# Loading the first key tile over ScalarE's queue, twelve products of ones on TensorE, and the first values ahead of the second pair

## The chip, the cores and the metric

The kernel runs on one core of one Trainium2 chip. The metric is the device time of one execution in microseconds (us). A core has engines that run side by side, each through its own list of instructions in order: TensorE (PE in the profile, its weight loads PEld), VectorE (DVE), ScalarE (ACT), GpSimd (POOL) and SyncE (SP). SyncE issues nearly all DMAs of this kernel; what it issues is carried out by 16 DMA engines. An engine waits for another one, or for a DMA, on a semaphore.

## The reference

```python
scores = np.matmul(q, k.transpose(0, 1, 3, 2)) / 8
scores = cap * np.tanh(scores / cap)
scores = scores - np.max(scores, axis=-1, keepdims=True)
attn = np.exp(scores)
attn = attn / (np.sum(attn, axis=-1, keepdims=True) + 1e-09)
x = np.matmul(attn, v)                  # (8, 12, 448, 64), then heads side by side: (8, 448, 768)
gate_pre[:, s] = sum over i of conv_w[i] * xp[:, s + i]      # xp is x with 4 zero rows ahead of it
out = (sigmoid(gate_pre) * (x @ w_val)) @ w_out
```

q, k and v are (8, 12, 448, 64) in float32; w_val and w_out (768 x 768) and conv_w (5 x 768) come as float64 and are taken apart into two float32 parts on the chip. cap is one number.

## The kernel before

Two heads make a pair p; there are 48 pairs, 6 in each of the 8 batches. For each pair, `load_blocks` (L165) brings q and k in four DMAs each, 32 rows of 14 blocks of 32 numbers a DMA, and `turn` (L289, its transposition L291) transposes them on VectorE, so that the 64 numbers of each of the two heads lie on partitions (`qt`, `kt`). The keys are cut into four tiles of 112. `scores` (L312) makes the scores of one key tile for both heads (`pss`, 112 x 896) with two matmuls side by side, each of which TensorE runs in two passes; `tanh` (L320) and `exp` (L324) are one ScalarE instruction each over such a tile; `attnv` (L349) multiplies by the values `vn`, which `load_v` (L184) brings in two DMAs, and `sums` (L361) by `ones`, which gives the sums of the softmax. Then VectorE turns the sums (`zt`, L369), inverts them and multiplies (`u`, L390), ScalarE copies the result (`xh`, L395), and the convolution (`gate`), the sigmoid and the two large products (`val`, `out_part`) follow.

Two score tiles fit into PSUM at a time (`ps_s` has two buffers). The work of all pairs is written in one order, sorted by due times: a table gives each step of pair p the time p + x, and the sorted list is what each engine executes, in order. The tables of the first six pairs (`EARLY`) put `scores` of pair p ahead of the end of pair p - 1. Into the same order come the weights: step n loads a piece of w_val or w_out (`weight_load`, `late_load`: `w_raw` and `w_late`), and takes it apart with two instructions on ScalarE (`weight_first`, L126 and L127) and several on VectorE (L130, L131, L134 to L136). The first of these steps is due at 0.70, and so stands on ScalarE behind the four `exp` of pair 0 and ahead of the `tanh` of pair 1. The small weights conv_w (`cw_raw`, five DMAs) stand just ahead of it.

The start is apart from this order. Ahead of it the kernel loads cap (`capt`) and the q and k of pair 0 (into `u2`, two buffers that are free until pair 0 is done: u0 for q and u1 for k), computes a flag from cap (`mag`, `small`), and every engine reads the flag (`TENSOR_LOAD`) and branches to `fast_path`. All other DMAs are issued behind the branch. A DMA reports on one of eight semaphores (DMAHW0 to DMAHW7), which are handed out in turn; an issue waits until the earlier DMA on its semaphore has landed.

Of the kernel before, what the change touches and what calls it, by code (L numbers as in the profile page):

```python
# [7 lines left out]
F32 = mybir.dt.float32  # L8
# [13 lines left out]
P = 128  # L22
ENG = mybir.EngineType

CH = 112
# [73 lines left out]
W_SECOND, W_THIRD, W_THIRD_EARLY = 0.02, 0.05, 0.71  # L99
W_FREE = 11.3  # L100
CW_LOAD, CW_AT = -0.55, 0.6
EPS = 1e-9


# [57 lines left out]
    return make  # L162


def load_blocks(nc, t, src, p):  # L165


    _, H, S, D = src.shape
    b, hp = divmod(p, H // 2)
    for g in range(P // BLK):  # L170
        j, d = divmod(g * BLK, D)
        nc.sync.dma_start(
            t[g * BLK:(g + 1) * BLK].rearrange("p (c e) -> p c e", e=BLK),
            src[b, 2 * hp + j, :, d:d + BLK].rearrange("(c r) e -> r c e", r=BLK),
        )


# [7 lines left out]
    return vn  # L185


def fast_path(tc, io, u2, q, k, v, w_val, conv_w, w_out, out, capt):

# [19 lines left out]
    with ExitStack() as ctx:  # L211
# [21 lines left out]
        nc.vector.scalar_tensor_tensor(guard, capt, -1.0, capt, ALU.mult, ALU.min)  # L233
        nc.scalar.activation(guard, guard, AF.Exp)
        nc.vector.tensor_scalar_mul(guard, guard, EPS)  # L235
        ones = cpool.tile([P, D], F32, name="ones")
        nc.gpsimd.memset(ones, 1.0)
        cw = cpool.tile([P, NCC, KW], F32, name="cw")

        for t in u2:  # L240
# [43 lines left out]
        def load(name, src, p):  # L284
            if p:
                loads[name, p] = io.tile([P, S], F32, name=name + "n")
                load_blocks(nc, loads[name, p], src, p)

        def turn(name, p):  # L289
            t = wk.tile([P, S], F32, name=name + "t")  # L290
            nc.vector.transpose(t, loads.pop((name, p)))  # L291
            state.setdefault(p, {})[name] = t

        def half_hi(name, p):
# [58 lines left out]
        def sums(p, i):  # L353

            st = state[p]
            n = len(tables[p]["sums"])
            if i == 0:
                st["z"] = bank(p, "psz")
            t = st["p" if n == NKT else "a", i]
            for j, r in enumerate(ROWS):  # L360
                nc.tensor.matmul(st["z"][r, :S], ones[:CH], t[:, j], start=(i == 0), stop=(i == n - 1))  # L361
            if i == n - 1:
                vloads.pop(p)

# [131 lines left out]
        for p, table in enumerate(tables):  # L496
            for name, f in steps.items():
                x = table.get(name, ())
                if isinstance(x, tuple):
                    for i, y in enumerate(x):  # L500
                        at(p + y, f, p, i)
                else:
                    at(p + x, f, p)
        for b in range(B):
            t0 = NPAIR * b
            for d in range(NCC):
# [157 lines left out]
def kernel(tc, q, k, v, cap, w_val, conv_w, w_out, out):  # L664
    nc = tc.nc
    with tc.tile_pool(name="cap_pool", bufs=1) as pool, tc.tile_pool(name="io", bufs=2) as io:
        capt = pool.tile([P, 1], F32, name="capt")
        nc.sync.dma_start(capt, cap.rearrange("(o c) -> o c", o=1).partition_broadcast(P))

        pad = conv_w.shape[0] - 1  # L670
        u2 = [pool.tile([P, pad + q.shape[2]], F32, name=f"u{i}") for i in range(2)]
        for t, src in zip(u2, (q, k)):
            load_blocks(nc, t[:, pad:], src, 0)
        mag = pool.tile([1, 1], F32, name="mag")
        nc.vector.scalar_tensor_tensor(mag, capt[0:1], -1.0, capt[0:1], ALU.mult, ALU.max)
        small = pool.tile([1, 1], I32, name="small")
        nc.vector.tensor_scalar(small, mag, CAP_FAST, None, ALU.is_le)
        flag = nc.values_load(small, min_val=0, max_val=1)
        with tc.If(flag != 0) as cmp:
            fast_path(tc, io, u2, q, k, v, w_val, conv_w, w_out, out, capt)  # L680
        with cmp.Else():
            general_path(tc, q, k, v, w_val, conv_w, w_out, out, capt)

# [29 lines left out]
```

## Time and profile before

| | |
|---|---|
| median of 3 runs | 750.18 us (749.81, 750.18, 752.12) |
| the profiled execution | 749.64 us |
| its span in the profile, from the first to the last instruction | 747.9 us |
| TensorE matmuls | busy 724.3 us, 97% of the span |
| VectorE | 593.0 us, 79% |
| ScalarE | 537.7 us, 72% |
| DMA, mean over the span | 85 GB/s; 241820 packets, 228448 of them under 512 B |

The profile is of one execution. Busy shares are averages over the whole span; the change touches the first 15 us, in which the engines stand in other proportions. All times that follow are counted from the start of the span. In rows of the timeline a bracket at the end gives how long the engine was idle ahead of the instruction and what released it by the profile's reading.

### The profile page before, as it was taken

The page shows a single profiled execution, that of the slowest core. Times are in us where ns is not written, and L with a number is a line of the kernel's source. Part 1 is how long each engine was busy: PE and PEld are TensorE (multiplying, and loading weights), DVE is VectorE, ACT ScalarE, POOL GpSimd, SP SyncE. Part 2 cuts the span into 40 slices and gives each one's busy share as a digit, 9 for nine tenths or more (in the row PEclk, how much of TensorE's full clock was granted, in tenths as well). Part 3 has the DMA queues.
Part 4 walks back from the last instruction along what each step waited for, and adds up shares of the span by engine and source line. Part 5 has one row for each costly group of instructions (what it writes and reads, how often), then busy time and mean ns, then how long its engine had stood idle before and what let it go on. Part 6 is the DMA issues. An engine that isn't in the chain of part 4 may idle for free.

```text
span 747.9 us, 10860 instructions
## 1 busy us (share of the span) xinstructions
PE 724.3 (97%) x3972; PEld 488.3 (65%) x3972; DVE 593.0 (79%) x972; ACT 537.7 (72%) x708; POOL 9.0 (1%) x16
## 2 busy tenths in 40 slices
PE   5899998999999999999999999999999999999997
PEld 2333655566667776676777766667667775775997
DVE  2799899888987789987998679988898778997320
ACT  5899967778776697677857677687976659674311
POOL 0000001000000000000000000000000000000000
PEclk9999999999999999999999999999999999999999
DMA  6998867853223232233322333233322332210001
GB/s 105 234 212 195 209 166 149 232 110 73 37 51 79 70 73 37 61 82 71 67 46 61 88 69 54 38 81 73 59 49 62 80 79 41 49 35 22 22 21 67
DMA packets 241820, 63.75 MB, mean 85 GB/s; under 512 B 228448, under 2 KB 235616, under 8 KB 241760
## 3 DMA queue, kind: packets, MB, share of 16 engines
q1 hardware_dynamic: 241760, 62.98, 38.1%
q8 instruction: 33, 0.54, 0.3%
q14 instruction: 27, 0.22, 0.1%
HBM read 51.94 MB, written 11.01 MB: 84 GB/s over the span
## 4 chain that ended last, share of the span: by engine, by line
PE 43%; DVE 25%; ACT 16%; issue 4%; SPq 1%; DMA 1%; DVEq 0%; ACTq 0%
PE psf L461 8%; PE pss L312 7%; PE psf L463 7%; PE psf L462 7%; PE psa L349 6%; DVE pa L334 5%; ACT pt L320 5%; ACT pt L324 4%; DVE gate L411 4%; PE psz L361 3%; ACT gate L417 2%; PE psf L432 2%; DVE g_l L226 2%; PE psf L433 2%; PE psf L434 2%
## 5 line engine op out<-in xcount | busy, mean ns | idle before, releaser
L320 ACT ACTIVATE pt<-pss,rc 112x896 f32<-112x896 f32 x192 | 185.6, 1003 | 28.7 <-PE pss L312 28.7
L324 ACT ACTIVATE pt<-pt,capt 112x896 f32<-112x896 f32 x192 | 189.2, 1038 | 0.1
L349 PE MATMUL psa<-pt,vn 112*64 112x448 f32 x720 | 146.9, 546 | 0.0
L411 DVE SCALAR_TENSOR_TENSOR gate<-u,cw,gate 128x448 f32<-128x448 f32 x192 | 132.4, 690 | 5.8
L461 PE MATMUL psf<-wo,g_h 128*128 128x384 f32 x336 | 117.6, 350 | 0.0
L463 PE MATMUL psf<-wo,g_l 128*128 128x384 f32 x336 | 113.3, 337 | 0.0
L462 PE MATMUL psf<-wo,g_h 128*128 128x384 f32 x336 | 113.2, 337 | 0.0
L432 PE MATMUL psf<-xh,wv 128*128 128x448 f32 x288 | 108.8, 378 | 0.1
L434 PE MATMUL psf<-xl,wv 128*128 128x448 f32 x288 | 104.4, 362 | 0.0
L433 PE MATMUL psf<-xh,wv 128*128 128x448 f32 x288 | 104.3, 362 | 0.0
L334 DVE TENSOR_TENSOR pa<-pt 112x896 f32<-112x896 f32 x84 | 91.1, 1084 | 13.3 <-ACT pt L324 13.3
L349 PEld LDWEIGHTS psa<-pt,vn 112*64 112x64 f32 x720 | 47.4, 136 | 81.2 <-issue 69.8
L395 ACT CAST xh<-u 128x448 fp32r<-128x448 f32 x48 | 27.1, 565 | 77.1 <-DVE u L390 77.0
L461 PEld LDWEIGHTS psf<-wo,g_h 128*128 128x128 f32 x336 | 63.4, 189 | 22.0 <-issue 17.7
L369 DVE STREAM_TRANSPOSE zt<-psz 128x448 f32<-128x448 f32 x45 | 28.9, 641 | 56.3 <-PE psz L361 56.3
L432 PEld LDWEIGHTS psf<-xh,wv 128*128 128x128 f32 x288 | 54.0, 187 | 25.9 <-issue 18.3
L463 PEld LDWEIGHTS psf<-wo,g_l 128*128 128x128 f32 x336 | 63.6, 189 | 0.3
L462 PEld LDWEIGHTS psf<-wo,g_h 128*128 128x128 f32 x336 | 63.6, 189 | 0.0
L312 PE MATMUL pss<-qt,kt 64*112 64x448 f32 x208 | 49.6, 593 | 13.4 <-DVE guard L235 7.9
L441 ACT CAST g_h<-gate 128x448 fp32r<-128x448 f32 x48 | 26.3, 562 | 47.4 <-DVE gate L438 47.3
L469 ACT COPY osb<-psf 128x384 f32<-128x384 f32 x56 | 26.7, 478 | 45.9 <-PE psf L463 43.2
L312 PE MATMUL pss<-qh,kh 64*112 64x448 f32 x280 | 58.5, 412 | 0.0
(74 smaller groups left out, 904.2 us busy)
## 6 DMA issues: line engine op xcount, KB each, us to landing
vn<-in_v_dram SPq DMA_DIRECT2D x96, 112.0 KB, 2.6
out_dram<-osb SPq DMA_DIRECT2D x56, 192.0 KB, 1.9
qn<-in_q_dram SPq DMA_DIRECT2D x188, 56.0 KB, 2.5
kn<-in_k_dram SPq DMA_DIRECT2D x188, 56.0 KB, 2.4
w_raw<-in_moe_w_val_dram SPq DMA_DIRECT2D x12, 384.0 KB, 4.5
w_late<-in_moe_w_val_dram SPq DMA_DIRECT2D x12, 384.0 KB, 4.3
w_raw<-in_moe_w_out_dram SPq DMA_DIRECT2D x12, 384.0 KB, 3.7
w_late<-in_moe_w_out_dram SPq DMA_DIRECT2D x12, 384.0 KB, 4.7
```

What stands on the lines that cost most here:

```text
L312: nc.tensor.matmul(ps[:CH, j, :S], st[x][r, c], st[y][r], start=(n == 0), stop=(n == len(parts) - 1))
L320: nc.scalar.activation(st["p", i], st.pop(("s", i)), AF.Tanh, scale=rc8[:CH])
L324: nc.scalar.activation(t, t, AF.Exp, scale=capt[:CH])
L334: nc.vector.tensor_tensor(st["a", i], st["p", 2 * i], st["p", 2 * i + 1], op=ALU.add)
L349: nc.tensor.matmul(st["o"][r, :S], vloads[p][:, j, i], t[:, j], start=(i == 0), stop=(i == NKT - 1))
L411: nc.vector.scalar_tensor_tensor(g, u[:, i:i + S], cw[:, hp, i:i + 1], g, ALU.mult, ALU.add)
L432: nc.tensor.matmul(o, w_h, xh, start=(c == 0), stop=False)
L433: nc.tensor.matmul(o, w_l, xh, start=False, stop=False)
L434: nc.tensor.matmul(o, w_h, xl, start=False, stop=(c == NCC - 1))
L461: nc.tensor.matmul(o, g_h[:, d, s], w_h, start=(d == 0), stop=False)
L462: nc.tensor.matmul(o, g_h[:, d, s], w_l, start=False, stop=False)
L463: nc.tensor.matmul(o, g_l[:, d, s], w_h, start=False, stop=(d == NCC - 1))
```

## The change

Four things are changed, all of them at the start.

1. q of pair 0 is loaded as before. Of the 14 blocks of its keys, the first 4 (128 keys) are issued by ScalarE, in four DMAs that stand ahead of ScalarE's reading of the flag; the other 10 blocks are issued by SyncE behind q.
2. The transposition of these keys is cut in two, 128 and 320 columns.
3. `ones` is made by VectorE as its first instruction (128 x 128 instead of GpSimd's 128 x 64 behind the branch), and TensorE multiplies it by itself twelve times into a bank of PSUM that nobody reads, ahead of its reading of the flag.
4. Behind the branch, the two DMAs of the first `vn` are issued ahead of the q and k of pair 1 instead of behind them.

```diff
+WARM, FIRST = 12, 4
-def load_blocks(nc, t, src, p):
+def load_blocks(eng, t, src, p, part=slice(None)):
...
-        nc.sync.dma_start(
-            t[g * BLK:(g + 1) * BLK].rearrange("p (c e) -> p c e", e=BLK),
-            src[b, 2 * hp + j, :, d:d + BLK].rearrange("(c r) e -> r c e", r=BLK),
+        eng.dma_start(
+            t[g * BLK:(g + 1) * BLK].rearrange("p (c e) -> p c e", e=BLK)[:, part],
+            src[b, 2 * hp + j, :, d:d + BLK].rearrange("(c r) e -> r c e", r=BLK)[:, part],
...
-        ones = cpool.tile([P, D], F32, name="ones")
-        nc.gpsimd.memset(ones, 1.0)
...
-            nc.vector.transpose(t, loads.pop((name, p)))
+            n = loads.pop((name, p))
+            cut = BLK * FIRST if name == "k" and not p else S
+            nc.vector.transpose(t[:, :cut], n[:, :cut])
+            if cut < S:
+                nc.vector.transpose(t[:, cut:], n[:, cut:])
...
-                    at(p + x, f, p)
+                    at(-2 if name == "load_v" and not p else p + x, f, p)
...
-        for t, src in zip(u2, (q, k)):
-            load_blocks(nc, t[:, pad:], src, 0)
+        load_blocks(nc.sync, u2[0][:, pad:], q, 0)
+        load_blocks(nc.scalar, u2[1][:, pad:], k, 0, slice(0, FIRST))
+        load_blocks(nc.sync, u2[1][:, pad:], k, 0, slice(FIRST, None))
+        ones = pool.tile([P, P], F32, name="ones")
+        nc.vector.memset(ones, 1.0)
+        with tc.tile_pool(name="ps_warm", bufs=1, space=PSUM) as ps_warm:
+            t = ps_warm.tile([P, 512], F32, name="warm")
+            for _ in range(WARM):
+                nc.tensor.matmul(t[:, :P], ones, ones, start=True, stop=True)
```

SyncE's list from its first DMA up to its first DMA behind the branch, before (u_63 is the buffer of q, u_64 that of k; the size is rows x blocks x numbers, and "waits" names the semaphores):

```order
L668 DMA capt<-in_cap_dram 128x1
L172 DMA u_63<-in_q_dram 32x14x32 x4
L172 DMA u_64<-in_k_dram 32x14x32 x3
L172 DMA u_64<-in_k_dram 32x14x32 [waits DMAHW0_49]
L678 TENSOR_LOAD small [waits DVE_49]
L678 ISA x2
L679 COMPARE_AND_BRANCH
L172 DMA qn<-in_q_dram 32x14x32 [waits DMAHW1_49]
```

And now:

```order
L673 DMA capt<-in_cap_dram 128x1
L174 DMA u_63<-in_q_dram 32x14x32 x3
L174 DMA u_63<-in_q_dram 32x14x32 [waits DMAHW0_49]
L174 DMA u_64<-in_k_dram 32x10x32 [waits DMAHW1_49]
L174 DMA u_64<-in_k_dram 32x10x32 [waits DMAHW2_49]
L174 DMA u_64<-in_k_dram 32x10x32 [waits DMAHW3_49]
L174 DMA u_64<-in_k_dram 32x10x32 [waits DMAHW4_49]
L692 TENSOR_LOAD small [waits DVE_49]
L692 ISA x2
L693 COMPARE_AND_BRANCH
L186 DMA vn<-in_v_dram 112x4x64 [waits DMAHW5_49]
```

The number of issues ahead of the branch is still nine, four of them smaller. Four of the eight semaphores now serve ScalarE's issues, so SyncE's waits begin at the fourth q instead of the fourth k; VectorE's transposition of q waits for DMAHW6, 7, 3 and 0 and its first part of the keys for DMAHW5, 4 and 2, which makes DMAHW0 in the third row the first of ScalarE's four.

SyncE's list behind the branch, up to the first piece of the large weights, before:

```order
L172 DMA qn<-in_q_dram 32x14x32 x4
L172 DMA kn<-in_k_dram 32x14x32 x4
L184 DMA vn<-in_v_dram 112x4x64 x2
L146 DMA cw_raw<-in_moe_conv_w_dram 128x6x2 x5
L258 DMA w_raw<-in_moe_w_val_dram 128x768 x2
```

And now:

```order
L186 DMA vn<-in_v_dram 112x4x64 x2
L174 DMA qn<-in_q_dram 32x14x32 x4
L174 DMA kn<-in_k_dram 32x14x32 x4
L148 DMA cw_raw<-in_moe_conv_w_dram 128x6x2 x5
L258 DMA w_raw<-in_moe_w_val_dram 128x768 x2
```

The values moved from ninth to first place; what stands ahead of `cw_raw` and of `w_raw` is the same fifteen issues.

TensorE's list from its start to the first product with the values, before:

```order
L678 TENSOR_LOAD small [waits DVE_49]
L679 COMPARE_AND_BRANCH
L312 MATMUL pss<-qt,kt 112x448 [waits DVE_49]
L312 MATMUL pss<-qt,kt 112x448 x3
L312 MATMUL pss<-qt,kt 112x448 [waits Activation_49]
```

And now:

```order
L687 MATMUL warm<-ones 128x128 [waits DVE_49]
L687 MATMUL warm<-ones 128x128 x11
L692 TENSOR_LOAD small [waits DVE_49]
L693 COMPARE_AND_BRANCH
L316 MATMUL pss<-qt,kt 112x448 [waits DVE_49,PE_49]
L316 MATMUL pss<-qt,kt 112x448
L316 MATMUL pss<-qt,kt 112x448 [waits DVE_49]
```

The twelve products stand ahead of the reading of the flag, and the second score tile has a wait of its own, for the second part of the keys. On ScalarE nothing behind the branch changes its place.

## Rows read from the trace of the kernel before

**Rows 1.** The page: busy time of each engine, and the last chain's shares.
```profile
PE 724.3 (97%) x3972; PEld 488.3 (65%) x3972; DVE 593.0 (79%) x972; ACT 537.7 (72%) x708; POOL 9.0 (1%) x16
...
PE 43%; DVE 25%; ACT 16%; issue 4%; SPq 1%; DMA 1%; DVEq 0%; ACTq 0%
```

**Rows 2.** ScalarE's timeline, 9 to 40 us: start, duration, operation, idle and releaser.
```profile
9.80 1.01 ACT L320 ACTIVATE pt<-pss,rc 112x896 f32<-112x896 f32 x1 [3.90 <-PE pss L312]
11.29 1.01 ACT L320 ACTIVATE pt<-pss,rc 112x896 f32<-112x896 f32 x1 [0.49 <-PE pss L312]
...
18.02 0.23 ACT L127 ACTIVATE cw_raw<-cw_raw 128x30 f32<-128x30 f32 x1
19.72 0.92 ACT L126 ACTIVATE w_t<-w_raw 128x768 f32<-128x768 f32 x1 [1.47 <-DMA w_raw<-in_moe_w_val_dram]
...
36.80 0.56 ACT L395 CAST xh<-u 128x448 fp32r<-128x448 f32 x1 [1.45 <-DVE u L390]
```

**Rows 3.** SyncE's timeline, 0 to 25 us.
```profile
0.75 0.39 SPq L668 DMA_DIRECT2D capt<-in_cap_dram  x1
1.21 1.98 SPq L172 DMA_DIRECT2D u<-in_q_dram  x4
3.23 2.04 SPq L172 DMA_DIRECT2D u<-in_k_dram  x4
6.27 1.88 SPq L172 DMA_DIRECT2D qn<-in_q_dram  x4
...
10.28 1.01 SPq L184 DMA_DIRECT2D vn<-in_v_dram  x2
11.33 2.93 SPq L146 DMA_DIRECT2D cw_raw<-in_moe_conv_w_dram  x5
14.30 1.02 SPq L258 DMA_DIRECT2D w_raw<-in_moe_w_val_dram  x2
...
22.76 1.01 SPq L184 DMA_DIRECT2D vn<-in_v_dram  x2
```

**Rows 4.** Issue to landing: tiles u (0 to 8 us), w_raw (13 to 16), vn (22 to 28).
```profile
DMA to landing us min/median/max: 2.3/2.4/2.6
...
DMA to landing us min/median/max: 4.4/4.6/4.7
...
DMA to landing us min/median/max: 2.8/2.9/2.9
```

**Rows 5.** Timeline of TensorE and VectorE, 19 to 37 us.
```profile
20.90 0.92 PE L361 MATMUL psz<-pt,ones 112*64 112x448 f32 x4
...
22.56 1.91 PE L312 MATMUL pss<-qt,kt 64*112 64x448 f32 x8 [0.74 <-ACT pt L320]
...
25.81 1.27 PE L349 MATMUL psf<-pt,vn 112*64 112x448 f32 x4 [1.35 <-ACT xh L395]
...
34.23 0.65 DVE L369 STREAM_TRANSPOSE zt<-psf 128x448 f32<-128x448 f32 x1 [1.35 <-PE psf L361]
```

**Rows 6.** All waits of ScalarE from 36 to 75 us: total, times, longest.
```profile
ACT xh L395 <- DVE u L390: 1.5, 1, 1.5
```

**Rows 7.** Timeline of the start on VectorE and TensorE.
```profile
5.22 0.65 DVE L291 STREAM_TRANSPOSE qt<-u 128x448 f32<-128x448 f32 x1 [0.48 <-DMA u<-in_q_dram]
...
7.91 5.90 PE L312 MATMUL pss<-qt,kt 64*112 64x448 f32 x16 [7.91 <-DVE guard L235]
```

**Rows 8.** Line 312, 7 to 14 us: ns of a weight load, min/median/max.
```profile
L312 PEld LDWEIGHTS pss<-qt,kt x16: 258/307/308, 7.9 to 12.5; 64*112 64x112 f32 x16
```

**Rows 9.** The page's groups: busy us and mean ns of one, idle before.
```profile
L461 PEld LDWEIGHTS psf<-wo,g_h 128*128 128x128 f32 x336 | 63.4, 189 | 22.0 <-issue 17.7
```

**Rows 10.** TensorE's busy time (instructions), granted clock and DMA, by windows.
```profile
689.10:692.50 3.40, 3.40 (x13) 0.50 0.00 0
692.50:696.00 3.50, 3.50 (x21) 1.00 0.15 56
```

**Rows 11.** TensorE's timeline ahead of the first of these windows.
```profile
687.51 0.97 PE L361 MATMUL psz<-pa,ones 112*64 112x448 f32 x4 [1.72 <-DVE pa L331]
```

More of the change, by code (lines that the diff above doesn't have):

```diff
@@ L185, in load_v, with fast_path @@
     return vn
-def fast_path(tc, io, u2, q, k, v, w_val, conv_w, w_out, out, capt):
+def fast_path(tc, io, ones, u2, q, k, v, w_val, conv_w, w_out, out, capt):
     nc = tc.nc
@@ L286, in load @@
                 loads[name, p] = io.tile([P, S], F32, name=name + "n")
-                load_blocks(nc, loads[name, p], src, p)
+                load_blocks(nc.sync, loads[name, p], src, p)
         def turn(name, p):
             t = wk.tile([P, S], F32, name=name + "t")
-            nc.vector.transpose(t, loads.pop((name, p)))
+            n = loads.pop((name, p))
[3 more added lines that the diff above has]
+                nc.vector.transpose(t[:, cut:], n[:, cut:])
             state.setdefault(p, {})[name] = t
@@ L360, in sums @@
             for j, r in enumerate(ROWS):
-                nc.tensor.matmul(st["z"][r, :S], ones[:CH], t[:, j], start=(i == 0), stop=(i == n - 1))
+                nc.tensor.matmul(st["z"][r, :S], ones[:CH, :D], t[:, j], start=(i == 0), stop=(i == n - 1))
             if i == n - 1:
@@ L679 @@
         with tc.If(flag != 0) as cmp:
-            fast_path(tc, io, u2, q, k, v, w_val, conv_w, w_out, out, capt)
+            fast_path(tc, io, ones, u2, q, k, v, w_val, conv_w, w_out, out, capt)
         with cmp.Else():
```

## The prediction

> **What bounds the kernel now.** I read the page first: TensorE is busy for 724.3 of 747.9 us, and the chain that ended last runs over TensorE, VectorE and ScalarE by turns [rows 1]. These are averages over the whole span. The change touches only the first 15 us, so the question is which wait of that stretch reaches the end. For that I follow ScalarE from its first tanh on, then the queue that feeds it.
>
> The first tanh starts at 9.80, having waited for TensorE, and the second at 11.29, 1.49 later and after a wait of 0.49 [rows 2]. The last instruction of this first block, on the small weights, ends at 18.25. Then ScalarE waits 1.47 us, until 19.72, for `w_raw`, the first piece of the large weights [rows 2]. This is the place that decides: ScalarE is already early there. In its list the tanh of pair 1 stand behind this step, and so all that follows hangs on the landing of `w_raw` and not on the first tanh.
>
> When does `w_raw` land? SyncE issues without a pause: q and k up to 5.27, the flag and the branch, and from 6.27 one DMA after the other, `w_raw` at 14.30 to 15.32 [rows 3]. Its two DMAs land 4.4 to 4.7 us after their issue [rows 4]; the second, issued near 14.9, makes 19.6. The landing is therefore the start of SyncE's list behind the branch, 6.27, plus a sum of issue times.
>
> The next wait is of the same kind. TensorE starts the values of pair 1 at 25.81 after 1.35 us of idle time [rows 5]. The bracket names ScalarE's copy, but these products need `vn` of pair 1, issued at 22.76 [rows 3] and landing 2.8 to 2.9 later [rows 4]: 25.6 to 25.7. I take the DMA for the releaser. From there the sums reach VectorE at 34.23, which waited 1.35 for them [rows 5], and its `u` reaches ScalarE at 36.80, which waited 1.45 [rows 2]. That is ScalarE's only wait from 36 to 75 us [rows 6]. So whatever shift stands at 36.80 is carried on by a full ScalarE for 38 us, and I see nothing to take it back.
>
> **The change, part by part.** *SyncE ahead of the branch.* Before, four issues of 448 runs take 1.98 to 2.04 us, 0.52 each with the gap; the 128-row issue of cap takes 0.39, some 0.44 with its gap [rows 3]. The smaller key issues have 320 runs and lie between: 0.47 each, or 0.2 us less for four. Against that the fourth q now waits for the first of ScalarE's DMAs. If ScalarE issues it when SyncE issues cap (0.75) and it lands after 2.3 to 2.6 us [rows 3, 4], this is at 3.05 to 3.35; before, this issue began at about 2.7. That is a delay of 0.35 to 0.65. Together SyncE reaches its branch later by about 0.3. Bounds: no wait and 0.44 for each key issue give 0.3 earlier; ScalarE's four issues (0.4 each) in the way of SyncE's own give 1.5 later. I take 0.3 later, as the waits in the list say, because no row shows two queues in each other's way.
>
> *Behind the branch.* The values go ahead of q and k: the same ten issues, so `cw_raw` and `w_raw` keep their distance from the branch. q and k of pair 1 land 1.0 us later; VectorE transposes them before 14 us and TensorE's scores of pair 1 come after that. Price nothing; without that cover it would be up to 1.0.
>
> *The front end.* q lands at 3.2 + 2.4 = 5.6 and is transposed by 6.3 (0.65 [rows 7]); the first 128 key columns take at most 128/448 of that, 0.2. So the keys of the first score tile are ready near 6.5 instead of 7.86. The twelve products run in 24 passes. A score tile, two passes of 448 columns, takes 1.49 cold, as the two tanh show [rows 2]; 128 columns then take 0.21 a pass, 5.1 us in all. They begin near 1.0, behind a memset of a fraction of a microsecond, and end near 6.1, sooner if the clock rises in between. Reading the flag and branching cost at most SyncE's 1.0 [rows 3]. First scores: near 6.9 instead of 7.91, and at the full clock a tile takes half, so the first tanh comes near 7.9 instead of 9.80. The second tile waits for the last of SyncE's key issues (begun near 5.2, landed 7.6, transposed by 8.1) and has its tanh near 9.2 instead of 11.29. The first block gains about 2 us and ends near 16.3, or when `cw_raw` is there.
>
> *Where these 2 us go.* Into the wait for `w_raw`: 1.47 becomes about 3.5. TensorE, done with pair 0 at 21.8 (20.90 + 0.92 [rows 5]), is done near 19.6. From the front end the end gains 0.0; from SyncE it is 0.3 later.
>
> *TensorE's clock.* TensorE's idle time ahead of the second half of the scores of pair 1 (22.56, 0.74 idle [rows 5]) grows to some 3 us. The trace has one fall of the clock after the start: 1.72 us of idle time ended at 687.51 [rows 11], and in 689.1 to 692.5 the granted clock is 0.50, the lower of its two levels; 13 matmuls run in 3.4 us, where the next 3.5 us hold 21 [rows 10]. The idle time of 1.35 at 24.46 did not bring it down. 3 us are longer than either, so I expect the fall. From restart to full clock it took 5.0 us there (687.51 to 692.5), and at the start of the kernel at least 4.6 (first matmul 7.91 [rows 7]; all weight loads up to 12.5 take 258 to 308 ns [rows 8], where a larger one takes 189 later [rows 9]). After a restart at 22.9 this gives a low clock until about 27.9. The scores have slack, since the values land only at 26.0; from 26.0 to 27.9 half of the time is lost, 0.9. Between nothing (no fall, or an early return) and 1.7 (a return at 29.4) I take 0.8.
>
> *The sum.* 749.64 (the profiled execution) + 0.0 + 0.3 + 0.8 = 750.7. That execution lies 0.54 below the median of three, 750.18, and within their spread; so the forecast is no change that a measurement of this kernel can tell from none (0.3%, 2.25 us).
>
> **A rule that speaks against the second queue.** No row has two engines issuing at once. The Trainium skill (DMA: Bandwidth & Descriptors, Issuing engines are not separate DMA queues) says that DMAs run on the same 16 DMA engines whoever starts them, and that a second issuing engine saves only the sequencer's time; its section Queues, rings and completion order adds that ScalarE and SyncE have no descriptor generator of their own. No run here shows this. By it the issues would take turns, which is the second rival below.
>
> **The rivals.**
> *Faster.* SyncE reaches the branch 0.3 earlier and the clock holds: 749.3. For it speaks that the key issues are smaller; against it the new wait of the fourth q. The whole 2 us of the front end would give 747.6, just past 0.3%, but need `w_raw` and `vn` 2 us earlier, and SyncE's list has at most 0.3 to give.
> *The issues take turns.* ScalarE's four issues delay SyncE's: 1.5 later at the branch, and with 0.8 for the clock 751.9. It decides if four issues of 0.4 fit into no gap of SyncE's 0.52 rhythm.
> *Slower, by TensorE's clock alone.* The clock falls late and comes back late, near 30.5: half of 26.0 to 30.5 is 2.3, with SyncE's 0.3 752.2. It takes more than 7 us from restart to full clock, more than the 5.0 that the trace shows; with a return after 31 it passes 0.3%.
> *The products don't do what they are there for.* If each pass also pays for its own weight load (0.31 cold [rows 8]), 24 passes take 12.5 us and end at 13.5; the flag stands behind them, so the first scores begin past 14. The first block then ends near 22.4, at the full clock, and the wait of 1.47 is used up: 2.7 later, 752.3. It decides if they end more than 3 us later than I expect. Against it: at the full clock a weight load takes 189 ns [rows 9] and yet 21 matmuls fit into 3.5 us [rows 10], 167 ns each, so the loads lie beside the matmuls.
>
> **How the numbers follow.** Forecast (front end absorbed, SyncE and clock within their nearer bounds) 0.50, with its own range 749.7 to 751.7; faster rival 0.17 (748.6 to 749.7, with 0.05 beyond 0.3%); issues taking turns 0.18 (751.5 to 752.6); slow clock 0.10; products in the way 0.05. Leaving out 2 in 10 at the ends gives 749.0 to 752.5. Slower by over 0.3% (752.43 and up): a quarter of the third case, half of the last two, and 0.02 of the forecast, together 0.14. Faster 0.05, the rest, 0.81, within 0.3%.
>
> **What the changed profile would show.** First tanh near 8, second near 9; ScalarE's wait ahead of line 128 (`w_t`) near 3.5 us, ended by the DMA, at 20.0; SyncE's first issue behind the branch at 6.6; `vn` of pair 1 issued at 23.1; TensorE idle for some 3 us near 20 to 23, then a stretch at granted clock 0.5; ScalarE's copy at 36.80 about 1 later. The prediction is wrong if the wait for `w_raw` does not grow, or if `w_raw` lands at another distance from the branch than 13.4 us.

## The result, and the profile after

The changed kernel takes 752.31 us (750.10 to 753.95, 14 runs) against 750.53 us (749.32 to 752.12, 14 runs) of the kernel before: ratio 1.0023, interval 1.0013 to 1.0033. That is 0.23% slower: clear of noise, inside the whole range of the forecast and within 0.3%, but 1.6 us above the 750.7 that was forecast. The profiled execution took 752.25 us, its span is 750.5 us (before: 749.64 and 747.9). Line numbers behind the branch are up to 4 higher after the change: the tanh is L324, the scores L316, the products with the values L353, `w_t` L128, the copy `xh` L399.

ScalarE's timeline of the changed kernel, as in [rows 2]; ACTq is its queue of DMA issues:

```profile
0.75 1.94 ACTq L174 DMA_DIRECT2D u<-in_k_dram  x4
...
7.92 1.01 ACT L324 ACTIVATE pt<-pss,rc 112x896 f32<-112x896 f32 x1 [1.97 <-PE pss L316]
9.47 1.01 ACT L324 ACTIVATE pt<-pss,rc 112x896 f32<-112x896 f32 x1 [0.54 <-PE pss L316]
...
17.17 0.23 ACT L128 ACTIVATE cw_t<-cw_raw 128x30 f32<-128x30 f32 x1 [1.18 <-DMA cw_raw<-in_moe_conv_w_dram]
...
20.00 0.89 ACT L128 ACTIVATE w_t<-w_raw 128x768 f32<-128x768 f32 x1 [2.27 <-DMA w_raw<-in_moe_w_val_dram]
...
38.10 0.56 ACT L399 CAST xh<-u 128x448 fp32r<-128x448 f32 x1 [2.20 <-DVE u L394]
...
139.36 0.90 ACT L128 ACTIVATE w_t<-w_raw 128x768 f32<-128x768 f32 x1 [1.14 <-DVE rc L380]
```

The first tanh starts 1.88 earlier than in [rows 2], the second 1.82. Ten microseconds later nothing is left: ScalarE waits 1.18 for `cw_raw` and 2.27 for `w_raw`, 3.45 in place of 1.47, and its step behind `w_raw` starts at 20.00, 0.28 later than before. The copy comes 1.30 later, and at 139.36 there is a wait that the kernel before doesn't have; there this step starts without one:

```profile
137.38 0.89 ACT L126 ACTIVATE w_t<-w_raw 128x768 f32<-128x768 f32 x1
```

The copy at 36.80 is that of pair 1; the one of pair 0 starts at 25.15. Some of the expectations below call it the copy of pair 0.

SyncE's timeline, as in [rows 3]:

```profile
1.20 2.90 SPq L174 DMA_DIRECT2D u<-in_q_dram  x4
4.14 1.99 SPq L174 DMA_DIRECT2D u<-in_k_dram  x4
7.12 0.85 SPq L186 DMA_DIRECT2D vn<-in_v_dram  x2
...
12.20 2.82 SPq L148 DMA_DIRECT2D cw_raw<-in_moe_conv_w_dram  x5
15.07 1.01 SPq L258 DMA_DIRECT2D w_raw<-in_moe_w_val_dram  x2
...
22.95 1.01 SPq L186 DMA_DIRECT2D vn<-in_v_dram  x2
```

Four issues of q take 2.90 instead of 1.98, and SyncE reaches its first issue behind the branch at 7.12 instead of 6.27. At `w_raw` it is still 0.77 late, at the values of pair 1 only 0.19.

TensorE's and VectorE's timelines, as in [rows 5] and [rows 7], and the windows, as in [rows 10]:

```profile
1.07 4.62 PE L687 MATMUL warm<-ones 128*128 128x128 f32 x24 [1.07 <-DVE ones L683]
6.87 1.01 PE L316 MATMUL pss<-qt,kt 64*112 64x448 f32 x4 [1.19 <-DVE kt L293]
...
18.86 0.92 PE L365 MATMUL psz<-pt,ones 112*64 112x448 f32 x4
22.77 3.33 PE L316 MATMUL pss<-qt,kt 64*112 64x448 f32 x8 [2.99 <-ACT pt L324]
26.04 2.11 PE L353 MATMUL psf<-pt,vn 112*64 112x448 f32 x4
...
35.54 0.65 DVE L373 STREAM_TRANSPOSE zt<-psf 128x448 f32<-128x448 f32 x1 [2.28 <-PE psf L365]
```

```profile
17.00:21.60 4.60, 2.78 (x16) 0.84 (x12) 1.53 (x7) 2.02 (x4) 0.23 (x1) 1.00 1.00 340
21.70:28.50 6.80, 5.73 (x15) 2.74 (x17) 6.47 (x12) 6.80 (x10) 0.00 (x0) 0.50 1.02 211
28.50:32.00 3.50, 3.50 (x20) 1.65 (x16) 3.39 (x6) 3.22 (x4) 0.00 (x0) 1.00 0.88 114
```

TensorE is done with pair 0 at 19.78, stands idle for 2.99 (before: 0.74), and from 21.7 to 28.5 the granted clock is 0.50. The eight score passes take 3.33 instead of 1.91, the first products with the values 2.11 instead of 1.27. The sums reach VectorE 1.31 later than in [rows 5].

Where the 2.6 us of span went, by the shift of ScalarE's instructions against the trace of before: +0.23 at the values of pair 1 (0.19 at their issue), +1.08 more while the clock is low (together the +1.30 at the copy), -0.56 between 90 and 97 us (before, VectorE waits 0.48 there for a `w_late`), +1.25 at 139.36, and +0.6 behind ScalarE's last instruction, whose cause stays open. The last three were in no step of the prediction. SyncE's timeline at that place, the time from issue to landing of the two `w_raw`, and the DMA queues from 133 to 135 (packets, MB, share of the 16 DMA engines):

```profile
133.49 1.69 SPq L258 DMA_DIRECT2D w_raw<-in_moe_w_out_dram  x2
```

```profile
DMA to landing us min/median/max: 3.3/4.4/5.4
```

```profile
q1 hardware_dynamic: 19, 0.06, 27.5%
q8 instruction: 1, 0.02, 2.7%
```

The same issue in the kernel before:

```profile
132.75 0.82 SPq L258 DMA_DIRECT2D w_raw<-in_moe_w_out_dram  x2
```

A DMA of another queue, "instruction", one packet of 16 KB, starts at 133.9, just when SyncE issues the second `w_raw`. This issue takes 1.29 us instead of 0.43, the DMA lands 5.4 us after it, and ScalarE waits. The bracket names VectorE's `rc`; the last chain runs over the DMA. In the kernel before the packet of this queue comes at 138.4, 5.7 us behind the first issue. These packets are called fetches from here on, because they follow the number of instructions that TensorE has worked off: at this one it has begun 589 passes in the kernel before and 586 in the changed one, of which 24 are the products of ones.

### The profile page after: what moved, and what is told of

Read it like the earlier page. It is cut to its first block, busy times and chain, and to the rows that moved or that the text cites. A ratio compares the mean times of both kernels' runs of the same rounds, so it can differ in the third digit from the quotient of the medians.

```text
span 750.5 us, 10915 instructions
## 1 busy us (share of the span) xinstructions
PE 729.1 (97%) x3996; PEld 493.7 (66%) x3996; DVE 593.4 (79%) x974; ACT 538.1 (72%) x708; POOL 8.9 (1%) x15
## 4 chain that ended last, share of the span: by engine, by line
PE 41%; DVE 22%; ACT 14%; issue 3%; DMA 1%; DVEq 0%; SPq 0%; ACTq 0%
PE psf L465 7%; PE pss L316 7%; PE psf L466 6%; PE psf L467 6%; PE psa L353 5%; DVE pa L338 5%; ACT pt L324 4%; ACT pt L328 4%; DVE gate L415 4%; ACT gate L421 2%; PE psz L365 2%; PE psf L436 2%; PE psf L437 2%; PE psf L438 2%; DVE g_l L228 2%
## 5 line engine op out<-in xcount | busy, mean ns | idle before, releaser
L324 ACT ACTIVATE pt<-pss,rc 112x896 f32<-112x896 f32 x192 | 185.7, 1003 | 26.8 <-PE pss L316 26.8
L353 PE MATMUL psa<-pt,vn 112*64 112x448 f32 x720 | 146.9, 546 | 0.0
L415 DVE SCALAR_TENSOR_TENSOR gate<-u,cw,gate 128x448 f32<-128x448 f32 x192 | 132.4, 690 | 5.8
L353 PEld LDWEIGHTS psa<-pt,vn 112*64 112x64 f32 x720 | 47.3, 136 | 81.0 <-issue 70.3
L399 ACT CAST xh<-u 128x448 fp32r<-128x448 f32 x48 | 27.1, 565 | 77.2 <-DVE u L394 77.1
L316 PE MATMUL pss<-qt,kt 64*112 64x448 f32 x208 | 48.7, 582 | 10.9 <-ACT pt L324 9.0
L316 PE MATMUL pss<-qh,kh 64*112 64x448 f32 x280 | 58.6, 412 | 0.0
```

Source lines behind the costliest of these rows:

```text
L316: nc.tensor.matmul(ps[:CH, j, :S], st[x][r, c], st[y][r], start=(n == 0), stop=(n == len(parts) - 1))
L324: nc.scalar.activation(st["p", i], st.pop(("s", i)), AF.Tanh, scale=rc8[:CH])
L353: nc.tensor.matmul(st["o"][r, :S], vloads[p][:, j, i], t[:, j], start=(i == 0), stop=(i == NKT - 1))
L415: nc.vector.scalar_tensor_tensor(g, u[:, i:i + S], cw[:, hp, i:i + 1], g, ALU.mult, ALU.add)
```

## The experiments

Theory A is the prediction's: the front end's gain goes into the waits for `w_raw` and the values, and what is lost is lost by TensorE's idle time and its clock. The rivals are told in each text, and the letters B and C change their meaning from one to the next. Two came from the profile after: C as it is meant from the wide filler on, that the mean granted clock alone tells the time, and D, that the moment of an instruction fetch decides whether a piece of the weights is late. Each ratio is to the kernel before on the same chip. No kernel leaves anything out; the fillers add products that nobody reads.

**The changed kernel again, and three parts undone.**

> The changed kernel once more, for a second profile and more times of it on the chip of this series. Every theory: ratio to before 1.0013 to 1.0033. Theory A: the clock falls near 21.7 and comes back near 28.5 in this profile too, and ScalarE's copy of pair 0 is again near 38.1. Theory D: the fetch at 133.9 and ScalarE's wait of 1.1 us at 139 are there again; if that wait is not there, the 1.25 us lost at 139 in the first profile was chance of that execution and not an effect of the change.

Measured: 752.15 us, ratio 1.0030 (1.0015 to 1.0044). Its profiled execution is the fastest of its twelve (750.52 us). ScalarE's and TensorE's rows in it, and the windows:

```profile
37.31 0.56 ACT L399 CAST xh<-u 128x448 fp32r<-128x448 f32 x1 [1.61 <-DVE u L394]
...
138.63 0.90 ACT L128 ACTIVATE w_t<-w_raw 128x768 f32<-128x768 f32 x1 [1.13 <-DVE rc L380]
```

```profile
22.91 3.02 PE L316 MATMUL pss<-qt,kt 64*112 64x448 f32 x8 [2.96 <-ACT pt L324]
26.32 1.27 PE L353 MATMUL psf<-pt,vn 112*64 112x448 f32 x4 [0.40 <-DMA vn<-in_v_dram]
```

```profile
19.90:23.20 3.30, 0.34 (x4) 0.27 (x4) 1.77 (x3) 3.03 (x4) 0.00 (x0) 1.00 1.22 260
23.30:26.60 3.30, 2.90 (x9) 0.87 (x6) 3.14 (x8) 3.30 (x6) 0.00 (x0) 0.50 0.88 152
```

The idle time is the same (2.96) and the clock falls again, but it is back at 26.7, when the products with the values have only begun (26.32): they wait for the values and start 0.51 late, the copy comes 0.51 late, and the clock costs nothing. So the 1.08 of the first profile is one draw of two. The wait at 139 is there again, 1.13, with the fetch at 132.7 and the issue at 132.77; both profiles of the changed kernel have it, and that of the kernel before does not. The fall near 690 that both first traces show [rows 10] is missing here, and ScalarE's last instruction starts where it did in the kernel before (743.15), though the last copy was still 1.56 late: that fall is worth 1.6 us, and is a draw too.

`WARM, FIRST = 0, 4` in place of `12, 4`:

> The changed kernel without the twelve products of ones (everything else as in the changed kernel). Theory A (the front end's gain is absorbed by the waits for w_raw and the values; what is lost is lost because TensorE falls idle for 3 us near 20 and its clock falls): TensorE starts cold, pair 0 is done near 20.6 instead of 19.78, the idle time ahead of the second half of the scores of pair 1 shrinks to some 2.2 us, the clock may still fall; 751.6 to 752.3, ratio to before 1.001 to 1.0025. Theory B (the products are what the change gains by; without them the first tanh come later and the end with them): first tanh near 8.7, time 1 us above the changed kernel, ratio 1.0035. Theory D (the moment of the instruction fetches, which depends on how many instructions TensorE has run, decides whether a piece of the weights is late): the fetches come some 0.5 to 1 us later, the wait for w_raw at 139 us is 1 us smaller or gone, the time 1 us below the changed kernel.

Measured: 751.12 us, ratio 1.0010 (0.9994 to 1.0027). The first tanh starts at 8.61, yet the step behind `w_raw` starts at 19.93 and the copy at 37.11: that the products bring a gain, falls. TensorE's idle time near 21 is 1.81, without a fall of the clock, and with the fetch at 140.1 there is no wait for `w_raw` at 139. But as much is lost elsewhere, 1.33 between the copies of pairs 1 and 6: a fetch at 61.2 comes while SyncE issues keys (5.48 us for the four, 2.62 in the changed kernel), ScalarE then waits 0.62 for a `w_raw` (at 73.36) and VectorE 0.93 for a `w_late` (at 92.60). The time is not resolved from the changed kernel's either, since the intervals overlap. What the products do is end pair 0 sooner, for nobody, and so make the idle time long.

`at(p + x, f, p)` again for the values of pair 0:

> The changed kernel with the values of pair 0 behind q and k of pair 1 again, as before the change. Theory A: what stands ahead of w_raw is the same, so w_raw lands at the same 19.95, and the time is that of the changed kernel within 0.3 us: ratio 1.0015 to 1.003. Rival: the values first make q and k of pair 1 land 1 us later and TensorE's scores of pair 1 with them; then undoing it gives back up to 1 us, ratio 1.001. Other rival: the values of pair 0, issued at 11.2, land after 14 and hold up TensorE's first products with them (13.4 in the changed kernel); then ratio 1.003 or more.

Measured: 751.57 us, ratio 1.0025 (1.0010 to 1.0041), the changed kernel's time. The values do land late, as the second rival said; in TensorE's timeline:

```profile
14.04 2.05 PE L353 MATMUL psa<-pt,vn 112*64 112x448 f32 x4 [2.50 <-DMA vn<-in_v_dram]
```

The clock falls there (14.2 to 17.6), and the copy of pair 0 is 1.47 late; but the step behind `w_raw` starts at 20.29, and the copy of pair 1 comes at 37.11: the waits for `w_raw` and for the values of pair 1 cover this too.

All keys of pair 0 on SyncE again:

```diff
-        load_blocks(nc.scalar, u2[1][:, pad:], k, 0, slice(0, FIRST))
-        load_blocks(nc.sync, u2[1][:, pad:], k, 0, slice(FIRST, None))
+        load_blocks(nc.sync, u2[1][:, pad:], k, 0)
```

> The changed kernel, with all keys of pair 0 issued by SyncE again; the twelve products, the values ahead of the second pair and the transposition in two parts stay. Theory A: SyncE's first issue behind the branch is back at 6.27 and the first piece of the large weights lands near 19.7 instead of 19.9; the first tanh comes near 8.7; TensorE still stands idle for 2 us or more ahead of the third score tile of pair 1 and its clock falls; the time lies 0.2 to 0.4 below the changed kernel's, ratio 1.0015 to 1.002. Rival B: the time is that of the kernel before, ratio 1.000. Rival C: 1.000 as well, with the low clock in the profile all the same.

Measured: 749.86 us, ratio 1.0006 (0.9991 to 1.0022). Theory A had expected 1.0015 to 1.002, and the rivals' 1.000 fits better. SyncE is behind its branch at 6.26, `w_raw` is issued at 14.31, and the copy comes at 36.22, 0.58 earlier than before the change.

```profile
19.18 0.92 ACT L128 ACTIVATE w_t<-w_raw 128x768 f32<-128x768 f32 x1 [1.44 <-DMA w_raw<-in_moe_w_val_dram]
```

By the median this part alone brings the time back, though the interval overlaps the changed kernel's. Two things differ at once, and the run does not part them: SyncE is not delayed, and the front end is slower (first tanh 9.27; the clock falls from 8.1 to 11.5 in spite of the products), so that TensorE's idle time near 21 is 1.14 and its clock stays there.

**Later weights: is the next wait there?** The weights' first step moved behind the tanh of pair 1:

```diff
-CW_LOAD, CW_AT = -0.55, 0.6
+CW_LOAD, CW_AT = -0.55, 1.22
-W_AT = (0.70, 1.70, ...
+W_AT = (1.25, 1.70, ...
...
+            third[0] = 1.45
```

> The changed kernel, with the steps on the small weights and on the first piece of the large ones moved on ScalarE and VectorE behind the first two tanh and exp of pair 1, so that ScalarE does not stand in the wait for the large weights; no DMA moves. Theory A: ScalarE's wait of 2.27 us at 20.00 is gone and its tanh of pair 1 start near 16.5 instead of 21.73, but TensorE's products with the values of pair 1 still start near 26, when these land, and the next copy comes near 37 to 38: the gain of the front end is taken up by the next wait, ratio 0.999 to 1.002. If instead the gain passes on from here, the ratio is near 0.996 to 0.997 (2 to 3 us). Rivals B and C expect no more than the first of these.

Measured: 752.92 us, ratio 1.0042 (1.0028 to 1.0057), slower than either branch of the expectation. The tanh of pair 1 start at 16.36 and the copy of pair 0 comes 2.30 earlier than before the change, so the wait for `w_raw` was what held them; the gain is gone at the next wait, TensorE's for the values of pair 1 (4.40 idle, until 26.32), and the clock falls. But the edit moves a DMA, which the expectation denied: the second `w_raw` is due behind the first step, and is issued at 29.49 instead of 24.07. SyncE and ScalarE:

```profile
29.49 0.90 SPq L258 DMA_DIRECT2D w_raw<-in_moe_w_val_dram  x2
```

```profile
34.09 0.93 ACT L128 ACTIVATE w_t<-w_raw 128x768 f32<-128x768 f32 x1 [5.88 <-DMA w_raw<-in_moe_w_val_dram]
```

The copy of pair 1 is 3.29 late by this wait, so the time of this run says nothing on theory A. With the values of pair 1 also issued ahead of the first `w_raw`:

> As the run with the weight steps later, and the two DMAs of the values of pair 1 issued ahead of the first large weights instead of behind the q and k of pair 2. Theory A: both waits that took up the front end's gain are out of its way; the values land near 18 instead of 26, the sums of pair 1 end near 29 to 31 instead of 35.5, the copy of pair 1 comes 3 or more us before 38.1, and the time falls by 2 to 4 us against the changed kernel: ratio to before 0.996 to 0.999. If the start does not reach the end at all (rival C), the ratio stays within 0.001 of the changed kernel's 1.0023.

Measured: 754.36 us, ratio 1.0055 (1.0036 to 1.0074), a miss. The second `w_raw` is late here too, issued only at 30.38, and ScalarE waits 7.44 us for it. Of the 6.3 us by which it is issued later than in the changed kernel, 5.4 stood in the run above already; a fetch at 22.2, during the four issues of the next keys, which take 5.27 us, is there for the rest at most. With two things moved at once it settles nothing on theory A.

**Filling the idle time.** Twelve products of ones ahead of the second half of the scores of pair 1, read by nobody:

```diff
+        def fill(n):
+            t = ps_f.tile([P, 512], F32, name="psf")
+            for _ in range(n):
+                nc.tensor.matmul(t[:, :P], ones, ones, start=True, stop=True)
...
+        at(0.9, fill, 12)
```

> The changed kernel, with twelve more products of ones on TensorE at the place where it now stands idle for 2.99 us (19.78 to 22.77, between the last sums of pair 0 and the third score tile of pair 1). They add work and no result. Theory A (the loss is the fall of TensorE's clock that this idle time brings): the clock stays at its upper level past 20 us, the sums of pair 1 end near 34.4 instead of 35.5, ScalarE's copy that came at 38.10 comes near 37.0, and the time falls by about 1.1 us: ratio to before near 1.001. Rival B (the loss is SyncE's later branch, 7.12 against 6.27, through its DMAs): the copy stays at 38.1 and the ratio at 1.0023. Rival C (what was measured comes from chance events far behind the start, as the wait of 1.14 us at 139): the copy may move, the ratio falls to 1.000 with or without the filler.

Measured: 754.11 us, ratio 1.0055 (1.0039 to 1.0070), which none of the three expected. The clock does stay at full speed past 20 us, and falls at 28.1 instead; SyncE's and TensorE's timelines show what came:

```profile
19.50 5.22 SPq L174 DMA_DIRECT2D kn<-in_k_dram  x4
24.77 1.01 SPq L186 DMA_DIRECT2D vn<-in_v_dram  x2
```

```profile
19.64 2.94 PE L482 MATMUL psf<-ones 128*128 128x128 f32 x24
22.66 1.91 PE L316 MATMUL pss<-qt,kt 64*112 64x448 f32 x8
27.75 2.05 PE L353 MATMUL psf<-pt,vn 112*64 112x448 f32 x4 [3.19 <-DMA vn<-in_v_dram]
```

The fetch, at 28.3 in the changed kernel, comes at 20.4, during the key issues; these take 5.22 instead of 3.54, and the values are 1.8 late. Six products with a last tile of pair 0 (`ones[:CH]`, 448 columns) put half as many instructions there:

> The changed kernel with six products of ones with the last tile of pair 0 (448 columns each, 12 passes, some 2.8 us) on TensorE ahead of the second half of the scores of pair 1; nobody reads them. They fill the idle time with half as many instructions as the first filler had. Theory A: the clock stays at full speed past 20 us, the scores at 22.7 take 1.9 instead of 3.3, ScalarE's copy of pair 0 comes at 37.0 instead of 38.1, and the time is 1.1 below the changed kernel: ratio to before 1.001. Theory C (the mean granted clock alone tells the time, 0.45 us for 0.001): mean clock 0.996, ratio 1.0005. Theory D: the instruction fetch moves from 28.3 to some 24 us; if it again meets the weights, SyncE's issue of a key load takes 2 us or more and the values of pair 1 land after 27: ratio 1.004 or more, as in the first filler.

Measured: 751.89 us, ratio 1.0028 (1.0011 to 1.0045), at a mean granted clock of 0.997. The fetch came at 20.1, not at 24, the key issues took 5.29, and the ratio lies between what theory A (1.001) and theory D (1.004) expected. So theory C falls: at the clock of the kernel before (0.996 to 0.997) this kernel is 2.2 us slower than it (749.70 in that series). The same filler, with six products of 256 columns at the start in place of twelve of 128, so that TensorE has run as many instructions as in the changed kernel:

> The changed kernel with the filler of six wide products ahead of the second half of the scores of pair 1, and six products of 256 columns at the start in place of twelve of 128: the same columns there, and TensorE runs as many instructions in all as in the changed kernel, so that its instruction fetch does not move to 20 us. Against the kernel with the wide filler and twelve products it tells what the moved fetch cost; against the changed kernel, what the fallen clock costs. Theory A with the clock as the cost: no fall near 21, scores at 22.7 in 1.9 us, values of pair 1 landed at 25.9, ScalarE's copy of pair 0 at 37.0, ratio to before 1.001. Theory D (the fetch): the fetch is back at 27 to 29 us, SyncE's four issues of the second key load take 2.1 us again, and the copy comes 2 us before that of the kernel with the wide filler (38.96). Rival C2 (the filler itself holds the scores up): copy at 38 or later with the fetch away from 20 us, ratio 1.0025.

Measured: 751.09 us, ratio 1.0003 (0.9985 to 1.0021). SyncE's key issues beside the wide filler, first with twelve products at the start, then with six:

```profile
19.40 5.29 SPq L174 DMA_DIRECT2D kn<-in_k_dram  x4
```

```profile
19.43 3.98 SPq L174 DMA_DIRECT2D kn<-in_k_dram  x4
```

With six the fetch is back at 28.7, and the copy comes at 37.65 (wide filler with twelve: 38.96; changed kernel: 38.10). So 1.31 us there go with the moment of one fetch. The copy is not at 37.0: with either start the filler took 4.78 us instead of 2.8 and pushed the scores to 24.3. In this profile the clock fell from 131.4 to 138.2, and 2.9 us were lost between the copies of pairs 6 and 9.

**Taking the absorber away.** The small weights' five issues on GpSimd's queue, in the changed kernel and in the kernel before:

```diff
     for i in range(kw):
-        nc.sync.dma_start(
+        nc.gpsimd.dma_start(
```

> The changed kernel with the five DMAs of the small weights issued by GpSimd, which is idle, instead of SyncE: they stand ahead of w_raw in SyncE's list and take 2.9 us there. Theory A (the 2 us that the front end gains go into the waits for w_raw and the values): w_raw is issued at 12.1 instead of 15.1 and lands at 17.0, ScalarE's step behind it starts near 17.2 instead of 20.0, the values of pair 1 land near 23 instead of 25.9, TensorE's idle time near 20 all but goes and the clock with it stays up; the copy of pair 0 near 35.0 instead of 38.1, and the time 2 to 3 us below the changed kernel, ratio to before 0.998 to 1.000. Rival (the next piece of the weights, w_late near 27 or the one at 90 us, takes the gain up): the copy near 35 to 36, but the same time, ratio 1.0015 to 1.003. Other rival (GpSimd's issues are slow, the small weights land behind 19): ScalarE waits for them instead, no gain.

> The kernel before with the five DMAs of the small weights on GpSimd. Theory A: here ScalarE is early by only 1.47 us at w_raw, so that is what can be gained: the step behind w_raw starts near 18.3 instead of 19.7, the copy of pair 0 near 35.4 instead of 36.8, ratio 0.998 to 0.9985; against the changed kernel with the same edit this gives what the change is worth when its gain has a way to the end: 1 to 1.5 us. Rival (a later piece of the weights takes it up): ratio 0.9995 to 1.001 for both.

Measured: 748.44 us, ratio 0.9976 (0.9961 to 0.9991), and 749.20 us, ratio 0.9989 (0.9970 to 1.0007). The changed kernel with this edit, on GpSimd, SyncE and ScalarE:

```profile
5.09 4.28 POOL L148 DMA_DIRECT2D cw_raw<-in_moe_conv_w_dram  x5 [0.44 <-issue]
```

```profile
12.21 0.95 SPq L258 DMA_DIRECT2D w_raw<-in_moe_w_val_dram  x2
...
131.27 1.51 SPq L258 DMA_DIRECT2D w_raw<-in_moe_w_out_dram  x2
```

```profile
17.18 0.93 ACT L128 ACTIVATE w_t<-w_raw 128x768 f32<-128x768 f32 x1 [0.44 <-DMA w_raw<-in_moe_w_val_dram]
...
34.54 0.56 ACT L399 CAST xh<-u 128x448 fp32r<-128x448 f32 x1 [1.24 <-DVE u L394]
...
136.84 0.89 ACT L128 ACTIVATE w_t<-w_raw 128x768 f32<-128x768 f32 x1 [0.83 <-DVE rc L379]
```

With `w_raw` issued 2.86 earlier the step behind it starts 2.82 earlier and the copy 3.56 earlier than in the changed kernel; the idle time of 2.99 is gone and the clock does not fall. The kernel before gains 1.65 at the step and 1.17 at the copy (35.63); its step now starts without a wait:

```profile
18.07 0.91 ACT L126 ACTIVATE w_t<-w_raw 128x768 f32<-128x768 f32 x1
```

Theory A is shown here at the copy: where both kernels have this edit, the change brings it 1.09 earlier instead of 1.30 or 0.51 later. That is a little more than half of the front end's 1.88; at 17.18 ScalarE waits 0.44 for `w_raw` again. As a time the 0.76 us between the two medians are not resolved, since the intervals overlap. The Trainium skill (DMA: Bandwidth & Descriptors, Issuing engines are not separate DMA queues) says that another issuing engine saves only the sequencer's time, usually little beside the DMA itself; by the rows it saves just that, but here the five issues are 2.8 to 2.9 us of SyncE's list [rows 3], and the landing of `w_raw` hung on them.

Of the 2.26 us that this copy has over the kernel before, 0.7 are lost again by pair 6 and 1.5 from 127 to 143 us, with a fetch at 131.3 and the issue of `w_raw` at 131.27. At pair 9 nothing of them is left; that this profile is the faster one all the same (748.60 us) comes from the fall of the clock near 690, which it doesn't have. So the last kernel has the same edit, and six products of 256 columns in place of twelve of 128:

> The changed kernel with the small weights on GpSimd's queue and six products of 256 columns at the start in place of twelve of 128: the same columns, but TensorE has run 24 passes' instructions less by any later point (12 products in place of 24 passes). Theory D (the moment of the fetch decides): near 131 us the fetch, which in the kernel with twelve products comes within 0.1 us of the issue of w_raw (131.3) and makes its second issue 1.1 us long, comes 2 to 3 us behind it; that issue takes 0.43 us again, ScalarE's wait of 0.8 us for w_raw at 136.8 is gone, the copy of pair 9 comes 1 to 1.5 us earlier than 143.3, and the time is 747.2, ratio to before 0.996. Rival (the fetch has nothing to do with it): the wait of 0.8 us is there again and the ratio is that of the kernel with twelve products, 0.9976.

Measured: 747.66 us, ratio 0.9971 (0.9959 to 0.9983). The fetch comes at 133.5, and SyncE's row at that place is

```profile
129.96 0.82 SPq L258 DMA_DIRECT2D w_raw<-in_moe_w_out_dram  x2
```

The issue takes 0.82 again, the wait at 137 is gone, and the copy of pair 9 comes at 141.1 instead of 143.3. Theory D is shown for this wait. But of the 2.14 us only 0.88 come between pairs 6 and 9; 1.26 stood at pair 6 already, most of them at a `w_late` near 89, for which VectorE waits 1.19 with twelve products and 0.18 with six. And 0.70 are still lost between pairs 6 and 9: the fetch now comes behind the issue of a `w_late`, which lands 6.2 us after its issue instead of 4.8 in the kernel before, and VectorE waits for it.

```profile
138.54 0.56 DVE L136 TENSOR_SCALAR w_late<-w_late 128x768 int32<-128x768 int32 x1 [0.56 <-DMA w_late<-in_moe_w_out_dram]
```

At pair 9 this kernel is 0.40 ahead of the kernel before with the same edit (2.09 against 1.69). As a time the gain over the twelve products is not resolved, since the intervals overlap.

All fourteen profiles: the copies of pairs 1, 6 and 9, in us against the kernel before (36.80, 97.07, 143.23), with the issue of that `w_raw`, its length, and the fetch next to it:

| kernel | pair 1 | pair 6 | pair 9 | `w_raw` issued | took | fetch | clock low before 700 us |
|---|---|---|---|---|---|---|---|
| before | 0 | 0 | 0 | 132.8 | 0.82 | 138.4 | 689.1 to 692.5 |
| changed | +1.30 | +0.74 | +2.00 | 133.5 | 1.69 | 133.9 | 21.7 to 28.5, 690.7 to 694.1 |
| changed, second profile | +0.51 | 0.00 | +1.53 | 132.8 | 1.54 | 132.7 | 23.3 to 26.7 |
| no products | +0.31 | +1.64 | +1.67 | 134.4 | 0.82 | 140.1 | none |
| values second | +0.31 | -0.27 | +2.32 | 132.5 | 1.37 | 132.4 | 14.2 to 17.6, 130.3 to 137.1 |
| all keys on SyncE | -0.58 | -1.13 | +0.36 | 131.6 | 0.82 | 132.2 | 8.1 to 11.5, 130.9 to 134.3 |
| weights later | +3.29 | +2.76 | +4.42 | 135.5 | 1.53 | 135.5 | 25.3 to 32.1, 134.5 to 137.9 |
| weights later, values earlier | +4.01 | +4.76 | +5.70 | 137.6 | 1.81 | 137.6 | 29.1 to 32.5, 39.3 to 42.7, 694.7 to 698.1 |
| filler of twelve | +3.63 | +3.05 | +5.80 | 135.8 | 1.65 | 136.2 | 28.1 to 31.5, 133.9 to 140.7 |
| wide filler | +2.16 | +2.35 | +2.63 | 135.2 | 1.28 | 135.1 | none |
| wide filler, same count | +0.85 | +0.27 | +3.18 | 133.1 | 0.82 | 133.6 | 131.4 to 138.2 |
| before, small weights on GpSimd | -1.17 | -1.71 | -1.69 | 131.1 | 0.82 | 136.8 | 687.5 to 690.9 |
| changed, small weights on GpSimd | -2.26 | -1.53 | +0.05 | 131.3 | 1.51 | 131.3 | none |
| the same, six wide products | -2.46 | -2.79 | -2.09 | 130.0 | 0.82 | 133.5 | none |

Between pairs 6 and 9 two things cost time, a fetch at the issue (length over 0.82) and a low clock between 130 and 141. With neither, four profiles lose 0.00 to 0.70; with the fetch alone, five lose 0.28 to 1.58; with the low clock alone, two lose 1.49 and 2.91; with both, three lose 1.66 to 2.75. The low clock there is the larger price, and five of the twelve profiles that have a part of the change show it, neither of the two without it; so few can't tell whether the change makes it likelier.

## Why the prediction came out as it did

*The range: held, in part by luck.* The median, 752.31, lies outside the forecast's own case (749.7 to 751.7) and in the band that the prediction gave to the issues taking turns (751.5 to 752.6), which were not seen. No change that a measurement can tell from none was forecast; 14 runs do tell it.

*The front end absorbed: right.* The tanh at 7.92 and 9.47 (forecast 7.9 and 9.2), the waits of 3.45 together (3.5), the step at 20.00 (20.0). That it was absorbed, and not worthless, the edit on GpSimd's queue shows, with 1.09 at the copy. That the values' DMA released TensorE at 25.81, and not the copy, fits the second profile, whose bracket names it (26.32).

*SyncE ahead of the branch: mechanism right, size off.* 0.85 later instead of 0.3. The wait of the fourth q for the first of ScalarE's DMAs was seen; that DMA landed 3.0 us after its issue (3.77) and not after 2.3 to 2.6, so the issue began at 3.79 instead of 3.05 to 3.35. The smaller key issues took 0.50 with their gaps, and saved 0.05 instead of 0.2.

*Behind the branch: w_raw's distance was wrong, in the kernel's favour.* From SyncE's first issue to the step it is 12.9 us instead of 13.4; the two DMAs land 3.9 to 4.3 us after their issue instead of 4.4 to 4.7 [rows 4]. The prediction named this as a sign of being wrong, and it kept the too large delay of SyncE harmless: 0.28 at the step. Why they land sooner stays open. Without ScalarE's issues, without the products and with the values second the median is 4.0 to 4.2, so none of these three is the cause alone.

*The clock: right, and a draw.* The fall was expected after 3 us of idle time, with a price of 0.8 between 0 and 1.7; the first profile has 1.08, the second none. The fall came inside the idle time in the first (21.7, restart at 22.8) and behind the restart in the second (23.3, restart at 22.9).

*The issues taking turns: not seen.* ScalarE's four issues took 0.42 to 0.49 us each while SyncE issued, and SyncE's first three q kept their rhythm. SyncE's delay is a wait on a semaphore. Taking turns was the prediction's own inference, and no run bears it out. That the DMAs share the engines, which is what the Trainium skill states (DMA: Bandwidth & Descriptors, Issuing engines are not separate DMA queues), fits: SyncE's first three q landed 2.9 to 3.1 us after their issue, and 2.4 to 2.6 where all keys were on SyncE.

*What failed: that whatever shift stands at 36.80 is carried on, and nothing takes it back.* Between 90 and 97 us almost 0.6 are taken back in both profiles, and at the step near 139 some 1.25 are added in both: the twelve products are 24 passes more in TensorE's instructions, the fetch comes 4.5 to 5.7 us earlier there, and it meets the issue of `w_raw`. With the 0.6 at the end, which stay open, that is most of what the sum lacked. The sum for the first profile is 749.64 + 0.23 + 1.08 - 0.56 + 1.25 + 0.6 = 752.2.

The runs as a whole agree with the clock as one part of the loss: the mean granted clock over the runs is 0.992 for the changed kernel (14 runs) and 0.996 for the kernel before (20 runs of the next series), and among the 14 runs the time falls by 0.45 us for each 0.001, which for that difference makes 1.8. This is a correlation, and in the other series of twelve runs or more it is 0.2 to 0.9 for each 0.001; how much of the 1.8 is the clock and how much the wait at 139 in the mean over runs, two profiles can't tell.

## What to carry to other kernels

Before a front end is made faster, follow its gain to the next thing that does not move with it; here that was the issuing queue. Taking 2.8 us of issues off it let the front end's gain through, 1.09 us of it at the copy; it is with this edit that the changed kernel is faster than the kernel before, by 0.24% and 0.29%. Added instructions can cost even where the engine is idle: they move the fetches of instructions, and these can meet a transfer 100 us later; moved away from one transfer, a fetch can meet the next. And an engine that is done early may lose its clock while it waits.

## What was not expected of the hardware

The fetches are single packets of 16 KB, 33 of them in a run, about 0.9 to 1.9 us each; smaller ones of 8 KB in the same queue were not followed. In 14 profiles the two issues of `w_raw` near 133 us took 1.28 to 1.81 us in the eight in which a fetch began between 0.1 before and 0.4 behind the first of them, and 0.82 in the six others, two of which had the fetch 0.5 behind the first of them.

Idle time alone does not tell whether the clock falls: in these 14 profiles 1.72 us of idle time ahead of 690 us were followed by a fall in four and by none in ten, 1.6 us near 130 by a fall in five and by none in nine, and 2.96 and 2.99 us near 21 by falls of 3.4 and 6.8 us. What one such fall costs is steady where nothing covers it: from the last copy to ScalarE's last instruction the ten profiles without the fall near 690 take 1.57 to 1.59 us less than the kernel before, the other three within 0.02 of it.
